# Sinkhorn attention followed by a two-layer feed-forward net on one core: the first dense layer begun early, pieces of the second layer's queue moved next to each other, one copy moved to another engine

**Chip, cores, metric.** One core of one Trainium2 chip. The time is device microseconds of that core, the median of several executions. A ratio is the mean time of one kernel's fast runs over the mean of the other kernel's fast runs of the same rounds, so it is not quite the ratio of the medians that are quoted.

## The reference

Four batches, eight heads, 768 positions, head width 64. Keys and values are mixed across eight blocks of 96 positions with a matrix P (five rounds of row and column normalising), attention is computed inside each block, and the result goes through a feed-forward net with 2048 inner features.

```python
k_sorted = np.einsum('bhij,bhjcd->bhicd', P, k_b).reshape(B, H, S, D)
v_sorted = np.einsum('bhij,bhjcd->bhicd', P, v_b).reshape(B, H, S, D)
scores = scale * np.matmul(q_b, k_sb.transpose(0, 1, 2, 4, 3))
attn = np.exp(scores - max) / sum
x = np.matmul(attn, v_sb)              # -> [3072, 512]
h = x @ w_in
r = np.maximum(h, 0.0)
out = (s * (r * r) + b) @ w_out
```

## The kernel before

TensorE does nearly everything, and the program fixes its order by hand. Each batch has two tiles (t = 2b and 2b + 1, 384 rows of x each). `ffn1(t)` is the first dense layer of a tile (tiles `hps`, `rt`, `gt`), `ffn2(t)` the second (`ops`, `ot`). While the second layer of one batch runs, a `Queue` slips in small pieces of the attention of the next, one piece after every four `ops` products:

- K pieces (`tk`, `ks`) mix keys; S pieces (`sc`, `at`) make scores and exponentials; P pieces (`pv`, `x`) apply them to the values; V pieces (`tv`, `vn`) mix values; q pieces (`tq`, `qt`) transpose q.
- K and S pieces use 64 of TensorE's 128 rows (forms 64\*128 and 64\*96 in the profile); `ops`, `hps`, q pieces and the V pieces of these queues use 128.
- A piece ends with copies out of PSUM on VectorE ("v") or ScalarE ("s").

```python
psa = ctx.enter_context(tc.tile_pool(name="psa", bufs=3, space=bass.MemoryType.PSUM))  # K, S, P, q, V2, hps
psb = ctx.enter_context(tc.tile_pool(name="psb", bufs=2, space=bass.MemoryType.PSUM))  # ops and small pieces

def k_piece(b, c0, nc2, nb, eng):
    pr = brows(b)[1] if nb == 1 else slice(0, 128)
    ...
        ps = psa.tile([128, nc2, nb * 64], FP, tag="a", name="tk")
    for c in range(nc2):
        nc.tensor.matmul(out=ps[:, c, :],
                         lhsT=kb[pr, c0 + 2 * c:c0 + 2 * c + 2, :].rearrange("p c d -> p (c d)"),
                         rhs=rhs, start=True, stop=True)
    ...                                # four casts into ks on engine eng

def bias_piece():                      # bias; then the first results of ffn2 may leave PSUM
    bps = psa.tile([128, 2, 512], FP, tag="a", name="bps")
    nc.tensor.matmul(out=bps[:, 0], lhsT=onesf, rhs=csum, start=True, stop=True)
    nc.vector.tensor_scalar(out=bias, in0=bps[:, 0], scalar1=b_bc, scalar2=None, op0=ALU.mult)
    ready.append(True)
    flush()

...                                    # end of the attention of tile 0
        warm_up(2, psa)
    t_part(0, 2, "v", 0, 2)
    warm_up(2, psa)
...
    V2 = [lambda c0=c0: v_piece2(c0, "s") for c0 in range(0, BLK, 16)]
    qu = Queue([nothing, lambda: q_piece(1, 2, "v")]
               + [lambda c0=c0: k_piece(1, c0, 16, 1, "vsv"[c0 // 32])() for c0 in range(0, BLK, 32)]
               + [seq(lambda: load_q(2), lambda: load_k(*brows(2)), bias_piece), V2[0], S2(2, 0), V2[1], S2(2, 2), V2[2], V2[3],
                  P2(2, 0), V2[4], P2(2, 2), V2[5], S2(3, 0),
                  seq(T(2), K(2, 0, 16, "s")), P2(3, 0), S2(3, 2), K(2, 32, 16, "s"), P2(3, 2), T(3),
                  seq(lambda: q_turn(2), K(2, 64, 16, "s"))], 24)
    ffn2(0, qu)
    ffn2(1, qu)
```

`load_q(2)` is six loads of 128 KB, `load_k` one of 768 KB; GpSimd issues both, after the `csum` sums that the bias needs. I call the queue above the **first queue** (second layer of batch 0) and the next one the **second queue** (second layer of batch 1).

The softmax here doesn't subtract the row's maximum and nothing guards it: scores larger than these inputs give would overflow.

Of the kernel before, what the change touches and what calls it, by code (L numbers as in the profile page):

```python
# [18 lines left out]
def kernel(  # L19
# [74 lines left out]
    def load_k(rows, prow, n=1):  # L94
        for c0 in range(0, BLK, BLK // n):
            cs = slice(c0, c0 + BLK // n)
            nc.gpsimd.dma_start(out=kb[prow, cs, :], in_=kraw[rows, cs, :])
# [4 lines left out]
    def brows(b):  # L102
        return slice(b * 64, (b + 1) * 64), slice((b % 2) * 64, (b % 2) * 64 + 64)
# [75 lines left out]
    def warm_up(n, pool=psb):  # L179
        wp = pool.tile([128, 256], FP, tag="b" if pool is psb else "a", name="wp")  # L180
        for _ in range(n):
            nc.tensor.matmul(out=wp, lhsT=zt[:, 0:128], rhs=zt, start=True, stop=True)  # L182
# [61 lines left out]
    def q_half(half, eng):  # L244

        if half == 0:
            QT[0] = qtp.tile([128, NHP, S], BF, tag="qt", name="qt0")
        pr = slice(half * 64, half * 64 + 64)
        ps = psa.tile([128, 2, 1024], BF, tag="a", name="tq")
        for hp in range(NHP):  # L250
            for t in range(TQ):
                c0 = (hp % 2) * TG + t * 64
                for e in range(2):
                    nc.tensor.transpose(out=ps[e * 64:(e + 1) * 64, hp // 2, c0:c0 + 64],  # L254
                                        in_=qr[0][pr, 2 * hp + e, t, :], identity=ident[pr, pr])
        for a in range(2):
            evac(QT[0][:, 2 * a:2 * a + 2, half * TG:(half + 1) * TG].rearrange(
                     "q b (p t) -> q b p t", t=TQ),
                 ps[:, a, 0:2 * TG].rearrange("q (b t p) -> q b p t", b=2, t=TQ), eng)

    def q_piece(b, hp0, eng):

        if hp0 == 0:
            QT[b] = qtp.tile([128, NHP, S], BF, tag="qt", name=f"qt{b}")
        ps = psa.tile([128, 2, 1024], BF, tag="a", name="tq")
        for i in range(2):
            for t in range(TQ):
                for e in range(2):
                    nc.tensor.transpose(
                        out=ps[e * 64:(e + 1) * 64, i, t * 128:(t + 1) * 128],  # L270
                        in_=qr[b][:, 2 * (hp0 + i) + e, t, :], identity=ident)
        evac(QT[b][:, hp0:hp0 + 2, :].rearrange("q a (p t) -> q a p t", t=TQ),
             ps[:, :, 0:S].rearrange("q a (t p) -> q a p t", t=TQ), eng)
# [8 lines left out]
    def k_piece(b, c0, nc2, nb, eng):  # L282




        pr = brows(b)[1] if nb == 1 else slice(0, 128)
        rhs = (pd1[pr] if b < 2 else pd2[pr, b - 2]).rearrange("p e m i -> p (e m i)")
        if nc2 * nb > 8:
            ps = psa.tile([128, nc2, nb * 64], FP, tag="a", name="tk")  # L290
        else:
            ps = psb.tile([128, nc2, nb * 64], FP, tag="b", name="tk")
# [4 lines that stand above are left out]
        g0 = (b % 2) * 32  # L297

        def half(cp):
            if b == 0:  # L300
                cs = slice(c0 + cp, c0 + 2 * nc2, 2)
            else:
                cs = slice(cp * (BLK // 2) + c0 // 2, cp * (BLK // 2) + c0 // 2 + nc2)
            for e in range(2):
                evac(ks[e * 64:(e + 1) * 64, g0:g0 + nb * 32, cs].rearrange(
                         "p (b g) c -> p b g c", b=nb),
                     ps[cp * 64:(cp + 1) * 64].rearrange(
                         "p c (b e g) -> p e b g c", b=nb, e=2)[:, e], eng)

        half(0)  # L310
        return lambda: half(1)
# [69 lines left out]
    def p_piece(t, hp, n0=0, nn=HB):  # L381
# [15 lines left out]
        for e in range(2):  # L397
# [11 lines left out]
            in0=pvv[:, :, :, 0:D],  # L409
            in1=rec[:, :, 0:nn].unsqueeze(3).broadcast_to([BLK, 2, nn, D]), op=ALU.mult)  # L410

    def t_piece(t, eng, n0=0, nn=HB):

        x = X[t]
        if t not in XT:
            XT[t] = xtp.tile([128, NHP, TG], BF, tag="xt", name="xt")
        if nn < HB:
            t1 = psb.tile([128, 1024], BF, tag="b", name="tr")
            tr = [t1[:, hp * nn * BLK:(hp + 1) * nn * BLK] for hp in range(NHP)]
            src = t1[:, 0:NHP * nn * BLK]  # L420
            dst = XT[t][:, :, n0 * BLK:(n0 + nn) * BLK]
            src = src.rearrange("p (a t) -> p a t", a=NHP)
        else:
            t2 = psa.tile([128, 2, 1024], BF, tag="a", name="tr")
            tr = [t2[:, hp // 2, (hp % 2) * TG:(hp % 2 + 1) * TG] for hp in range(NHP)]
            src = t2[:, :, 0:2 * TG]
            dst = XT[t].rearrange("p (a b) t -> p a (b t)", b=2)
        for hp in range(NHP):
            for n in range(n0, n0 + nn):
                nc.tensor.transpose(out=tr[hp][:, (n - n0) * BLK:(n - n0 + 1) * BLK],  # L430
                                    in_=x[:, n, hp * 128:(hp + 1) * 128],
                                    identity=ident[0:BLK, 0:BLK])
        evac(dst, src, eng)
# [27 lines left out]
    def nothing():  # L461
        pass

    def ffn1(t, slot=nothing, n0=0, nn=HB):
        if t not in GT:
            GT[t] = gtp.tile([128, NF, TG], BF, tag="gt", name="gt")
        gt = GT[t]
        c0, nt = n0 * BLK, nn * BLK
        for f0 in range(0, NF, 2):
            hps = psa.tile([128, 2, 512], FP, tag="a", name="hps")  # L470
            for f in range(2):
                for hp in range(NHP):
                    nc.tensor.matmul(out=hps[:, f, 0:nt], lhsT=wi_at(hp, f0 + f),  # L473
                                     rhs=xt_at(t, hp, n0, nn),
                                     start=(hp == 0), stop=(hp == NHP - 1))
            rt = rtp.tile([128, 2, TG], BF, tag="rt", name="rt")
            nc.scalar.activation(out=rt[:, :, 0:nt], in_=hps[:, :, 0:nt], func=AF.Relu)  # L477
            nc.vector.tensor_tensor(out=gt[:, f0:f0 + 2, c0:c0 + nt], in0=rt[:, :, 0:nt],  # L478
                                    in1=rt[:, :, 0:nt], op=ALU.mult)
            slot()  # L480
# [59 lines left out]
    def seq(*fs):  # L540
        def run():
            for f in fs:
                f()
        return run

    def S2(t, hp):
        return lambda: (s_piece(t, hp), s_piece(t, hp + 1))

    def P2(t, hp):
        return lambda: (p_piece(t, hp), p_piece(t, hp + 1))  # L550
# [53 lines left out]
            t_part(0, 0, "s", 0, 2)  # L604
        warm_up(2, psa)
    t_part(0, 2, "v", 0, 2)
    warm_up(2, psa)

    load_v(*brows(2))

# [1 line left out]
    def P(t, hp, *r):  # L612
        return lambda: p_piece(t, hp, *r)

    def SC(t, hp):
        return lambda: s_piece(t, hp)

    def V1(i, eng="s"):
        return lambda: v_piece1(i * 8, eng)

    ffn1(0, Queue([P(0, 0, 2, 2), P(0, 1, 2, 2), P(0, 2, 2, 2), P(0, 3, 2, 2),
                   lambda: q_half(1, "s"), lambda: t_piece(0, "v", 2, 2), SC(1, 0), SC(1, 1)], 8), 0, 2)
    ffn1(0, Queue([seq(SC(1, 2), P(1, 0)), V1(0), seq(SC(1, 3), P(1, 1)), V1(1), P(1, 2), P(1, 3),
                   seq(V1(2), V1(3)), lambda: t_piece(1, "v")], 8), 2, 2)
    V1(4)()
    V1(5)()
# [20 lines left out]
    def K(b, c0, nc2, eng):  # L647
        return lambda: k_piece(b, c0, nc2, 1, eng)()

    V2 = [lambda c0=c0: v_piece2(c0, "s") for c0 in range(0, BLK, 16)]  # L650
    qu = Queue([nothing, lambda: q_piece(1, 2, "v")]
               + [lambda c0=c0: k_piece(1, c0, 16, 1, "vsv"[c0 // 32])() for c0 in range(0, BLK, 32)]
               + [seq(lambda: load_q(2), lambda: load_k(*brows(2)), bias_piece), V2[0], S2(2, 0), V2[1], S2(2, 2), V2[2], V2[3],
                  P2(2, 0), V2[4], P2(2, 2), V2[5], S2(3, 0),
                  seq(T(2), K(2, 0, 16, "s")), P2(3, 0), S2(3, 2), K(2, 32, 16, "s"), P2(3, 2), T(3),
                  seq(lambda: q_turn(2), K(2, 64, 16, "s"))], 24)
    ffn2(0, qu)
    ffn2(1, qu)

# [6 lines left out]
    v_read(3, nc.gpsimd)  # L666
    load_q(3)
    qu = Queue([S2(4, 0), nothing, nothing, P2(4, 0), nothing, S2(4, 2), nothing, nothing,
                P2(4, 2), nothing, T(4), K(3, 0, 16, "v"), S2(5, 0), nothing, K(3, 32, 16, "s"),
                P2(5, 0), nothing, S2(5, 2), nothing, P2(5, 2), K(3, 64, 16, "s"), T(5),  # L670
                lambda: q_turn(3), nothing], 24)
    ffn2(2, qu)
    ffn2(3, qu)
# [39 lines left out]
```

## Time and profile before

| | before |
|---|---|
| time, median (range) | 233.32 us (233.07 to 233.37) |
| span in the profile | 231.6 us |
| TensorE busy | 224.3 us, 97% |
| VectorE / ScalarE / GpSimd busy | 50% / 49% / 21% |
| mean granted TensorE clock | 0.971 |

The chain that ended last, by engine, shows how much of the set time was not TensorE's own. ("q" after a name is the engine's sequencer.)

```profile
PE 82%; DVE 7%; DMA 5%; ACT 3%; issue 1%; POOL 0%; POOLq 0%
```

DVE's 7% is mostly the stretch that holds up the first results of the second layer. On TensorE's timeline it is one gap. The columns are start us, length us, engine, line, operation, out<-in, form, element type, count, and in brackets how long TensorE had been idle and what ended that.

```profile
69.18 0.73 PE L375 MATMUL sc<-qt,ks 64*96 64x96 bf16 x16
70.32 1.02 PE L516 MATMUL ops<-wo,gt 128*128 128x512 bf16 x4 [0.41 <-DVE ot L490]
```

A score block that should occupy 0.49 us occupies 1.14, because the next `ops` product needs a PSUM buffer that the first `ot` on VectorE frees. Throughout, I read **starts** of TensorE blocks: the lengths of matmuls are modelled and overlap what follows.

### The profile page before, as it was taken

How to read it: one execution, taken by the hardware profiler on the slowest of the kernel's cores; microseconds unless marked ns; L12 is line 12 of the kernel's file. 1: busy time of each engine (PE TensorE's matmuls, PEld its weight loads, DVE VectorE, ACT ScalarE, POOL GpSimd, SP SyncE). 2: the span in 40 equal slices, each digit the busy share in tenths (PEclk: the TensorE clock that was granted, in tenths of full speed). 3: DMA queues.
4: the chain of work that ended last, by engine and by line, in shares of the span. 5: the costliest groups of instructions: out<-in, count | busy, mean ns of one | idle time of the engine just before them, and what ended most of it. 6: DMA issues, size and time to landing. Idle time of an engine off the chain costs nothing.

```text
span 231.6 us, 4837 instructions
## 1 busy us (share of the span) xinstructions
PE 224.3 (97%) x2036; PEld 136.8 (59%) x2036; DVE 116.8 (50%) x245; ACT 114.6 (49%) x164; POOL 48.3 (21%) x62
## 2 busy tenths in 40 slices
PE   8879999999999999999999999999999999999994
PEld 6779887765544555566555555665555556554442
DVE  5778566638992645244446653343452634432221
ACT  6168479685158486856630645656222236660000
POOL 7820000399992000007920000000000000000000
PEclk9975699999999999999999999999999999999999
DMA  5999999998799992764999995610115240001212
GB/s 93 142 200 211 226 193 205 231 220 183 106 110 180 273 312 63 161 82 65 130 148 133 183 197 115 93 47 0 46 47 113 93 110 4 3 0 45 80 59 91
DMA packets 46695, 28.90 MB, mean 125 GB/s; under 512 B 35921, under 2 KB 41041, under 8 KB 46161
## 3 DMA queue, kind: packets, MB, share of 16 engines
q0 software_dynamic: 18800, 15.21, 47.8%
q1 hardware_dynamic: 27728, 13.32, 26.6%
q8 instruction: 16, 0.26, 0.5%
q10 hardware_dynamic: 144, 0.07, 0.1%
q14 instruction: 7, 0.05, 0.1%
HBM read 29.63 MB, written 8.65 MB: 165 GB/s over the span
## 4 chain that ended last, share of the span: by engine, by line
PE 82%; DVE 7%; DMA 5%; ACT 3%; issue 1%; POOL 0%; POOLq 0%
PE hps L473 35%; PE ops L516 31%; DMA qr<-in_q_dram 5%; PE pv L402 4%; PE sc L375 3%; DVE gt L478 2%; ACT ks L240 2%; DVE ks L238 2%; PE tv L320 2%; PE ops L501 2%; PE tk L294 1%; PE tv L350 1%; PE wp L182 1%; PE tq L254 1%; PE tv L336 1%
## 5 line engine op out<-in xcount | busy, mean ns | idle before, releaser
L473 PE MATMUL hps<-xt,wi 128*128 128x384 bf16 (+1 forms) x576 | 87.1, 309 | 0.3 <-ACT rt L477 0.3
L516 PE MATMUL ops<-wo,gt 128*128 128x512 bf16 x368 | 86.9, 380 | 0.4 <-DVE ot L490 0.4
L473 PEld LDWEIGHTS <-wi 128*128 128x128 bf16 x576 | 54.1, 98 | 30.6 <-issue 1.3
L477 ACT ACTIVATE rt<-hps 128x768 bf16<-128x768 f32 (+1 forms) x72 | 53.1, 741 | 37.4 <-PE hps L473 37.0
L478 DVE TENSOR_TENSOR gt<-rt 128x768 bf16<-128x768 bf16 (+1 forms) x72 | 41.2, 574 | 50.2 <-ACT rt L477 50.0
L516 PEld LDWEIGHTS <-gt 128*128 128x128 bf16 x368 | 33.6, 98 | 37.2 <-issue 1.0
L378 ACT ACTIVATE at<-sc 96x768 bf16<-96x768 f32 x32 | 24.4, 804 | 27.7 <-PE sc L375 27.7
L490 DVE SCALAR_TENSOR_TENSOR ot<-ops,s_bc,bias 128x512 f32<-128x512 f32 x23 | 17.1, 749 | 41.2 <-PE ops L516 41.2
L240 ACT CAST ks<-tk 64x512 bf16<-64x512 f32 (+1 forms) x32 | 18.6, 582 | 10.5 <-PE tk L294 10.2
L407 DVE TENSOR_TENSOR x<-pv,rec 96x512 bf16<-96x512 f32 (+1 forms) x36 | 22.6, 627 | 1.3
L639 POOL TENSOR_TENSOR csum<-csum,wo 128x512 f32<-128x512 f32 x14 | 17.6, 1254 | 1.0
L402 PEld LDWEIGHTS <-at 96*128 96x128 bf16 (+1 forms) x256 | 12.0, 104 | 3.8
L182 PE MATMUL wp<-zt 128*128 128x256 bf16 x86 | 12.9, 311 | 1.1 <-DVE warm L113 1.1
L238 DVE CAST ks<-tk 64x512 bf16<-64x512 f32 (+1 forms) x20 | 13.0, 651 | 1.1 <-PE tk L294 0.8
L402 PE MATMUL pv<-vs,at 96*128 96x66 bf16 (+1 forms) x256 | 13.0, 199 | 0.1
L240 ACT CAST vn<-tv 128x512 bf16<-128x512 f32 (+1 forms) x12 | 9.4, 799 | 7.2 <-PE tv L350 5.0
L375 PEld LDWEIGHTS <-ks 64*96 64x96 bf16 x256 | 8.6, 128 | 5.8 <-issue 5.1
L406 DVE RECIPROCAL rec<-pv 96x8 f32<-96x8 f32 (+1 forms) x36 | 6.9, 192 | 9.5 <-PE pv L402 9.4
L84 POOL DMA_DIRECT2D qr<-in_q_dram x12 | 10.6, 912 | 4.8 <-DMA kb<-in_k_dram 3.1
L375 PE MATMUL sc<-qt,ks 64*96 64x96 bf16 x256 | 10.9, 219 | 0.1
L182 PEld LDWEIGHTS <-zt 128*128 128x128 bf16 x86 | 9.0, 110 | 2.6 <-DVE warm L113 1.1
L294 PEld LDWEIGHTS <-kb 64*128 64x128 bf16 x192 | 6.7, 99 | 3.9 <-issue 3.4
(73 smaller groups left out, 98.4 us busy)
## 6 DMA issues: line engine op xcount, KB each, us to landing
out_dram<-ot SPq DMA_DIRECT2D x23, 256.0 KB, 2.4
kb<-in_k_dram POOLq DMA_DIRECT2D x4, 768.0 KB, 12.2
vb<-in_v_dram POOLq DMA_DIRECT2D x4, 768.0 KB, 19.0
wi<-in_moe_w_in_dram POOLq DMA_DIRECT2D x2, 1024.0 KB, 19.7
wo<-in_moe_w_out_dram POOLq DMA_DIRECT2D x2, 1024.0 KB, 32.6
qr<-in_q_dram POOLq DMA_DIRECT2D x12, 128.0 KB, 13.5
dv<-vn SPq DMA_DIRECT2D x6, 256.0 KB, 7.5
vs<-dv POOLq DMA_DIRECT2D x4, 384.0 KB, 12.7
```

Of the source, the lines that this page charges most:

```text
L182: nc.tensor.matmul(out=wp, lhsT=zt[:, 0:128], rhs=zt, start=True, stop=True)
L238: nc.vector.tensor_copy(out=out, in_=in_)
L240: nc.scalar.copy(out=out, in_=in_)
L375: nc.tensor.matmul(out=sc[:, e, n * BLK:(n + 1) * BLK], lhsT=ks[pr, g0 + n, :], rhs=QT[b][pr, hp, q0:q0 + BLK], start=True, stop=True)
L378: nc.scalar.activation(out=at, in_=sc[:, :, 0:TG], func=AF.Exp, scale=scale)
L402: nc.tensor.matmul(out=pv[e][0:m, (n - n0) * VW:(n - n0 + 1) * VW], lhsT=atf[:, c0:c0 + m], rhs=VS[b][:, gi, :], start=True, stop=True)
L407: nc.vector.tensor_tensor(out=x[:, n0:n0 + nn, hp * 128:(hp + 1) * 128].rearrange("p n (e d) -> p e n d", e=2), in0=pvv[:, :, :, 0:D], in1 ...
L473: nc.tensor.matmul(out=hps[:, f, 0:nt], lhsT=wi_at(hp, f0 + f), rhs=xt_at(t, hp, n0, nn), start=(hp == 0), stop=(hp == NHP - 1))
L477: nc.scalar.activation(out=rt[:, :, 0:nt], in_=hps[:, :, 0:nt], func=AF.Relu)
L478: nc.vector.tensor_tensor(out=gt[:, f0:f0 + 2, c0:c0 + nt], in0=rt[:, :, 0:nt], in1=rt[:, :, 0:nt], op=ALU.mult)
L516: nc.tensor.matmul(out=ops, lhsT=gt[:, f, m * 128:(m + 1) * 128], rhs=wo_at(f), start=(f == 0), stop=(f == NF - 1))
L639: nc.gpsimd.tensor_tensor(out=csum, in0=csum, in1=wo_at(f), op=ALU.add)
```

## The change

Its intent: (1) do useful products in place of two dummy warm-up products ahead of the first dense layer; (2) take a wait for a relu away; (3) put pieces that use 64 rows directly behind each other, so that TensorE changes its tiling (the form in which its rows and columns are divided) less often; (4) move the q copy from busy VectorE to idle ScalarE, so that bias and the first `ot` come earlier. An added function `p_pair` is never called and is left out here.

```diff
-    def ffn1(t, slot=nothing, n0=0, nn=HB):
+    def ffn1(t, slot=nothing, n0=0, nn=HB, lead=0):
 ...
+        for f0 in range(0, lead, 2):
+            begun[f0] = psa.tile([128, 2, 512], FP, tag="a", name="hps")
+            products(f0, begun[f0], range(0, NHP // 2))
         for f0 in range(0, NF, 2):
+            if f0 in begun:
+                hps = begun[f0]
+                products(f0, hps, range(NHP // 2, NHP))
 ...
     t_part(0, 2, "v", 0, 2)
-    warm_up(2, psa)
 ...
-                   lambda: q_half(1, "s"), lambda: t_piece(0, "v", 2, 2), SC(1, 0), SC(1, 1)], 8), 0, 2)
-    ffn1(0, Queue([seq(SC(1, 2), P(1, 0)), V1(0), seq(SC(1, 3), P(1, 1)), V1(1), P(1, 2), P(1, 3),
+                   lambda: q_half(1, "s"), lambda: t_piece(0, "v", 2, 2), SC(1, 0), SC(1, 1)], 8), 0, 2, 2)
+    ffn1(0, Queue([seq(SC(1, 2), P(1, 0)), V1(0), seq(SC(1, 3), P(1, 1)), P(1, 2), V1(1), P(1, 3),
 ...
-    qu = Queue([nothing, lambda: q_piece(1, 2, "v")]
-               + [lambda c0=c0: k_piece(1, c0, 16, 1, "vsv"[c0 // 32])() for c0 in range(0, BLK, 32)]
-               + [seq(lambda: load_q(2), lambda: load_k(*brows(2)), bias_piece), V2[0], S2(2, 0), ...
-                  P2(2, 0), V2[4], P2(2, 2), V2[5], S2(3, 0),
-                  seq(T(2), K(2, 0, 16, "s")), P2(3, 0), S2(3, 2), K(2, 32, 16, "s"), P2(3, 2), T(3),
-                  seq(lambda: q_turn(2), K(2, 64, 16, "s"))], 24)
+    qu = Queue([nothing, seq(lambda: q_piece(1, 2, "s"), K(1, 0, 16, "v")), nothing,
+                seq(K(1, 32, 16, "s"), K(1, 64, 16, "v")), nothing,
+                seq(lambda: load_q(2), lambda: load_k(*brows(2)), bias_piece),
+                V2[0], S2(2, 0), V2[1], S2(2, 2), V2[2], V2[3], P2(2, 0), V2[4], P2(2, 2), V2[5],
+                seq(T(2), S2(3, 0), K(2, 0, 16, "s")), nothing, P2(3, 0),
+                seq(S2(3, 2), K(2, 32, 16, "s")), nothing, P2(3, 2),
+                seq(T(3), lambda: q_turn(2)), K(2, 64, 16, "s")], 24)
 ...                                     # second queue
-                P2(4, 2), nothing, T(4), K(3, 0, 16, "v"), S2(5, 0), nothing, K(3, 32, 16, "s"),
-                P2(5, 0), nothing, S2(5, 2), nothing, P2(5, 2), K(3, 64, 16, "s"), T(5),
+                P2(4, 2), nothing, T(4), nothing, seq(S2(5, 0), K(3, 0, 16, "v")), nothing, nothing,
+                P2(5, 0), nothing, seq(S2(5, 2), K(3, 32, 16, "s")), nothing, P2(5, 2),
+                K(3, 64, 16, "s"), T(5),
```

More of the change, by code (lines that the diff above doesn't have):

```diff
@@ L410, in p_piece, with p_pair @@
             in1=rec[:, :, 0:nn].unsqueeze(3).broadcast_to([BLK, 2, nn, D]), op=ALU.mult)
+    def p_pair(t, hp0, n0):
+        b, half = divmod(t, 2)
+        if t not in X:
+            X[t] = xp.tile([BLK, HB, d_model], BF, tag="x", name="x")
+        p2 = psa.tile([128, 4, 256], FP, tag="a", name="pv")
+        for i in range(2):
+            atf = AT[t, hp0 + i].rearrange("p e t -> p (e t)")
+            for e in range(2):
+                for n in range(2):
+                    c0 = (e * HB + n0 + n) * BLK
+                    gi = e * 32 + (hp0 + i) * NB + half * HB + n0 + n
+                    nc.tensor.matmul(out=p2[:, 2 * i + e, n * VW:(n + 1) * VW],
+                                     lhsT=atf[:, c0:c0 + 128], rhs=VS[b][:, gi, :],
+                                     start=True, stop=True)
+        pvv = p2[0:BLK, :, 0:2 * VW].rearrange("p a (n w) -> p a n w", w=VW)
+        rec = rtp.tile([BLK, 4, 2], FP, tag="rec", name="rec2")
+        nc.vector.reciprocal(out=rec, in_=pvv[:, :, :, D])
+        nc.vector.tensor_tensor(
+            out=X[t][:, n0:n0 + 2, hp0 * 128:(hp0 + 2) * 128].rearrange(
+                "p n (a d) -> p a n d", d=D),
+            in0=pvv[:, :, :, 0:D], in1=rec.unsqueeze(3).broadcast_to([BLK, 4, 2, D]),
+            op=ALU.mult)
     def t_piece(t, eng, n0=0, nn=HB):
@@ L468, in ffn1, with products @@
         c0, nt = n0 * BLK, nn * BLK
-        for f0 in range(0, NF, 2):
-            hps = psa.tile([128, 2, 512], FP, tag="a", name="hps")
+        begun = {}
+        def products(f0, hps, part):
             for f in range(2):
-                for hp in range(NHP):
+                for hp in part:
                     nc.tensor.matmul(out=hps[:, f, 0:nt], lhsT=wi_at(hp, f0 + f),
@@ L475, in ffn1 @@
                                      start=(hp == 0), stop=(hp == NHP - 1))
+        for f0 in range(0, lead, 2):
+            begun[f0] = psa.tile([128, 2, 512], FP, tag="a", name="hps")
+            products(f0, begun[f0], range(0, NHP // 2))
+        for f0 in range(0, NF, 2):
+            if f0 in begun:
+                hps = begun[f0]
+                products(f0, hps, range(NHP // 2, NHP))
+            else:
+                hps = psa.tile([128, 2, 512], FP, tag="a", name="hps")
+                products(f0, hps, range(NHP))
             rt = rtp.tile([128, 2, TG], BF, tag="rt", name="rt")
@@ L650 @@
     V2 = [lambda c0=c0: v_piece2(c0, "s") for c0 in range(0, BLK, 16)]
-    qu = Queue([nothing, lambda: q_piece(1, 2, "v")]
-               + [lambda c0=c0: k_piece(1, c0, 16, 1, "vsv"[c0 // 32])() for c0 in range(0, BLK, 32)]
-               + [seq(lambda: load_q(2), lambda: load_k(*brows(2)), bias_piece), V2[0], S2(2, 0), V2[1], S2(2, 2), V2[2], V2[3],
-                  P2(2, 0), V2[4], P2(2, 2), V2[5], S2(3, 0),
-                  seq(T(2), K(2, 0, 16, "s")), P2(3, 0), S2(3, 2), K(2, 32, 16, "s"), P2(3, 2), T(3),
-                  seq(lambda: q_turn(2), K(2, 64, 16, "s"))], 24)
+    qu = Queue([nothing, seq(lambda: q_piece(1, 2, "s"), K(1, 0, 16, "v")), nothing,
[5 more added lines that the diff above has]
+                seq(T(3), lambda: q_turn(2)), K(2, 64, 16, "s")], 24)
     ffn2(0, qu)
```

## The prediction

> **What bounds the kernel now.** I read the page first. TensorE is busy nearly all the time, so the time is TensorE's instruction stream plus the few places where it stands still, and anything on another engine counts only if it makes TensorE stand still.
>
> ```profile
> span 231.6 us, 4837 instructions
> ...
> PE 224.3 (97%) x2036; PEld 136.8 (59%) x2036; DVE 116.8 (50%) x245; ACT 114.6 (49%) x164; POOL 48.3 (21%) x62
> ```
>
> Busy TensorE still hides two costs, so I went to TensorE's timeline and took starts only (ends are modelled and overlap the next start). The columns are start, length, engine and line, operation, out<-in.
>
> ```profile
> 79.75 1.03 PE L516 MATMUL ops<-wo,gt 128*128 128x512 bf16 x4
> 80.62 0.59 PE L350 MATMUL tv<-vb,pd 128*128 128x512 bf16 x2
> 81.05 1.03 PE L516 MATMUL ops<-wo,gt 128*128 128x512 bf16 x4
> 82.01 0.56 PE L375 MATMUL sc<-qt,ks 64*96 64x96 bf16 x16
> 82.50 1.04 PE L516 MATMUL ops<-wo,gt 128*128 128x512 bf16 x4
> 83.47 0.64 PE L294 MATMUL tk<-pd,kb 64*128 64x64 bf16 x16
> 84.04 1.04 PE L516 MATMUL ops<-wo,gt 128*128 128x512 bf16 x4
> 84.91 0.70 PE L402 MATMUL pv<-vs,at 96*128 96x66 bf16 x16
> ```
>
> Four ops products take 0.87 us when a 128-row piece follows (79.75 to 80.62) but 0.96 or 0.97 when a 64-row piece follows (81.05 to 82.01, 82.50 to 83.47): going into a 64-row piece costs 0.09. Single starts in the trace are 23.5 ns apart inside a score piece and 29.8 ns inside a key piece, so 16 take 0.38 and 0.48, while the blocks take 0.49 and 0.57: coming out costs about 0.10. The first ops gaps after it cost 0.01 more. One excursion into 64-row pieces thus costs **0.20 us**.
>
> The second cost is TensorE's waits. The chain of waits in order of time (start, length, what) shows three that the change touches:
>
> ```profile
> 42.45 0.50 ACT rt L477
> ...
> 61.48 1.67 DVE qt L238
> ...
> 68.73 0.76 DVE bias L561
> ...
> 69.52 0.76 DVE ot L490
> ...
> 70.32 1.02 PE ops L516 x4
> ...
> 85.92 0.59 ACT ks L240
> ...
> 86.55 0.56 PE sc L375 x16
> ```
>
> At 42.45 the hps product waits for a relu; the product before it ended a 0.23 us piece at 42.47 and it starts at 42.99, some 0.47 later than a free one. From 57 to 70 us the chain runs through VectorE: q copy, eight key casts, bias, first ot. The score block at 69.18 takes 1.14 us until 70.32 instead of 0.49: **0.65 us** lost. At 86.55 a score piece has waited 0.14 for a key cast on ScalarE.
>
> **What the Trainium skill says.** "TensorEngine Tiling (Array Packing)", Key Properties: "Changing tiling mode (not just tile) drains the TensorE". The trace agrees, with the 0.09 in and 0.10 out above; score and value pieces that alternate at 21 to 23 us, both 64-row, show no such gap. "SBUF — State Buffer", SBUF: two separate sides: VectorE instructions with two SBUF inputs and GpSimd instructions that read SBUF lock each other out. The trace agrees in kind: gt takes 0.56 us at 49.43 and 1.33 at 54.63 under the csum sums of GpSimd, which is why VectorE comes to its q copy only at 61.5. "TensorE: Matmul & The Clock Gate", Part 1: the clock is released on a free-running activity window, not by the kernel. In this trace the granted clock is 0.50 from 24.0 to 27.7 and 1.00 from 27.8. "DMA: Bandwidth & Descriptors", Queues, rings and completion order: each DMA engine takes turns between the queues that have work. This bears on a rival below.
>
> **The change part by part.**
>
> *First dense layer begun early.* Only one tile (two f) is begun on head pairs 0 and 1; p_pair is defined but never called.
>
> ```profile
> 26.57 0.53 PE L443 MATMUL tr<-ident,x 96*128 96x96 bf16 x4
> 26.90 0.63 PE L182 MATMUL wp<-zt 128*128 128x256 bf16 x2
> 27.32 1.05 PE L473 MATMUL hps<-xt,wi 128*128 128x192 bf16 x8
> 28.20 0.30 PE L402 MATMUL pv<-vs,at 96*128 96x66 bf16 x4
> ```
>
> The two warm-ups from 26.90 to 27.32 go. The four products on pairs 0 and 1 start at 26.90 (ScalarE's copy of that half is done at 26.87), 0.16 each at half clock, until 27.54; VectorE's copy of the other half is done at 27.49, so no wait. The 0.42 us saved is half-clock time: by 27.77 before had done 2.8 of 8 products, after has done 5.4, so it gains 2.6 at 0.083: **0.24 us**, if the clock rises at the same moment. The second half of wi landed at 30.4 (issued 7.9, 22.5 to landing), and is then asked for at 30.6 instead of 30.84: just in time.
>
> *v and value pieces swapped.* The wait of 0.47 goes, but P(1,2) now stands where V1(1) had given ScalarE and VectorE 0.4 us, so the next hps product should wait some 0.2 for the buffer of P(1,1). I count **0.2**.
>
> *Second layer, batches 1 and 2.* q and the first key piece share one excursion, but between two tilings there is still one drain: 0.12. Two key pieces together save one excursion: 0.20. The q copy (1.67 on VectorE, 1.44 as such a copy took at 47.19 on ScalarE) goes to an engine that idled from 59.0 to 63.8. VectorE then does two key pieces (8 casts, some 5.3 us) from 61.1: bias at about 66.4 to 67.2, first ot done by 68.0. TensorE wants that buffer at about 68.9, so the 0.65 is gone with some 0.9 to spare. Sum so far 0.24 + 0.2 + 0.12 + 0.20 + 0.65 = **1.4 us** at the score piece S2(3,0), which then starts at 80.6 instead of 82.0.
>
> *Key pieces behind score pieces.* Two in this queue and two in the next: 4 x 0.21 = 0.85, and the 0.14 at 86.55. In the second queue nothing waits, before or after: its inputs have landed (the transposes of q for batch 2 even go one place earlier). If nothing new waits, the sum is 1.4 + 0.85 + 0.14 = 2.4 us: 230.9.
>
> **The rivals.**
>
> *A. The key load takes the place of the waits removed.* K(2,0) needs the load of batch 2's keys:
>
> ```profile
> L97 POOL DMA_DIRECT2D kb<-in_k_dram x1: 594/594/594, 70.1 to 70.1; - x1
> ...
> DMA to landing us min/median/max: 12.3/12.3/12.3
> ```
>
> Issued at 70.15, landed at 82.4; before asks at 83.47, so 1.05 us of slack. The change asks right behind S2(3,0), at 80.6 + 0.4 = 81.0. Two things take the slack: 1.4 us of gain and one slot of four ops products. The load sits behind six q loads of small packets which follow the csum sums on GpSimd, perhaps 0.4 earlier after; but the DMA queues are full from 62 to 82 us and the ot and v stores come earlier too, so I expect it to land between 81.5 and 82.8, not a microsecond earlier. TensorE would then stand still for about 1.2 us. Sum for landing L: K starts at L + 0.05; the four ops products it used to follow are still to be done (0.86), so the gain there is 83.47 - L - 0.91. With L = 82.2 this is 0.36, and with what follows (0.14 + 0.21 + 0.43) it makes 1.14. I hold this the likeliest, 8 in 10.
>
> *B. ScalarE becomes the bound.* A score piece followed by a key piece puts 1.5 + 2.35 us on it at once, with three PSUM buffers all taken; the next value piece comes 1.7 us later, and the next score piece some 3.5. For: ScalarE is busy 20 of the 34 us from 58 to 92. Against: value pieces need the exponentials alone, which go first. At most 0.3 per place, so 231.5 to 232.5 with the other gains.
>
> *C. No gain at the start*, if the clock rises a window later or wi's second half lands later: lost 0.24 to 0.5, mostly hidden anyway if A holds, since the load sets the time in the middle.
>
> **Range and chances.** 233.3 - 1.1 = 232.2 with A; 230.9 without. Weighted with 8 to 2 the middle is 231.9; B may take some back, so I say **232.1**. The low end 230.8 is all gains with no new wait; the high end 233.2 is a load that lands at 82.8 or later and a wait on ScalarE. Two per cent is 4.7 us, twice the whole sum of gains: faster 0.03, same 0.95, slower 0.02.
>
> **What would show it.** First hps at 26.9 with four products ahead of the second copy; value piece at about 27.96. No 0.65 gap after the first score piece of batch 1 (the block about 0.49 long). Excursions of q with tk, tk with tk and sc with tk, with the second piece's first start about 0.03 behind in the like tilings and about 0.12 behind in q with tk. Under A, TensorE's weight load of tk waits for the DMA of kb by some 1.2 us at 81 to 82. I am wrong if that wait is absent (then near 230.9), if the load lands past 83 (then no gain), or if merged 64-row pieces still cost 0.09 each.

## The result, and the profile after

The median is **233.0 us** (232.95 to 233.38) against 233.34 for the kernel before in the same rounds (233.07 to 233.47): ratio 0.999 with a 95% interval of 0.9973 to 1.0008. Within 2%, inside the forecast range, but the gain is 0.3 us where 1.2 was forecast. All outputs were correct.

```profile
span 231.2 us, 4813 instructions
...
PE 222.2 (96%) x2014; PEld 136.6 (59%) x2034; DVE 115.8 (50%) x244; ACT 115.9 (50%) x165; POOL 48.2 (21%) x62
...
PE 91%; ACT 3%; DVE 3%; issue 1%; DVEq 0%
```

The busy time of TensorE fell by 2.1 us, the span by 0.4. Some 1.1 us of the 2.1 is only that 20 `ops` records are missing from this trace, so busy time can't say how much came back as standing still. I followed the starts of the same blocks in both traces:

| block start (us) | before | after | lead of the changed kernel |
|---|---|---|---|
| first `ops` of the second layer, batch 0 | 57.956 | 57.468 | 0.49 |
| S2(3,0), score piece | 82.007 | 80.556 | **1.45** |
| P2(3,0), value piece behind K(2,0) | 84.912 | 84.806 | **0.11** |
| S2(3,2), score piece | 86.548 | 86.301 | 0.25 |
| P2(3,2), value piece behind K(2,32) | 89.452 | 89.471 | -0.02 |
| first `hps` of tile 4 (behind the second queue) | 140.465 | 140.127 | 0.34 |
| last `ops` | 228.013 | 227.675 | 0.34 |

The gain was there, and it was lost at two places in 9 us. First what worked. The dense layer starts early, without the warm-ups:

```profile
26.49 0.49 PE L467 MATMUL tr<-ident,x 96*128 96x96 bf16 x4
26.84 1.07 PE L498 MATMUL hps<-xt,wi 128*128 128x192 bf16 x8
27.75 0.30 PE L402 MATMUL pv<-vs,at 96*128 96x66 bf16 x4
```

q and key piece follow each other, and the score block before the second layer's first `ot` is no longer held up (68.37 to 68.86 is 0.49):

```profile
59.29 0.86 PE L269 MATMUL tq<-ident,qr 128*64 128x128 bf16 x24
60.08 0.64 PE L294 MATMUL tk<-pd,kb 64*128 64x64 bf16 x16
...
68.37 0.56 PE L375 MATMUL sc<-qt,ks 64*96 64x96 bf16 x16
68.86 1.04 PE L552 MATMUL ops<-wo,gt 128*128 128x512 bf16 x4
```

Then what was lost, from the same timeline:

```profile
80.56 0.56 PE L375 MATMUL sc<-qt,ks 64*96 64x96 bf16 x16
82.50 0.64 PE L294 MATMUL tk<-pd,kb 64*128 64x64 bf16 x16 [1.38 <-ACT at L378]
83.07 1.90 PE L552 MATMUL ops<-wo,gt 128*128 128x512 bf16 x8
84.81 0.70 PE L402 MATMUL pv<-vs,at 96*128 96x66 bf16 x16
...
86.30 0.56 PE L375 MATMUL sc<-qt,ks 64*96 64x96 bf16 x16
87.16 0.64 PE L294 MATMUL tk<-pd,kb 64*128 64x64 bf16 x16 [0.30 <-DVE x L407]
87.73 1.90 PE L552 MATMUL ops<-wo,gt 128*128 128x512 bf16 x8
```

K(2,0) should start about 0.39 after the score piece's start, K(2,32) likewise. The first starts 1.94 later: 1.55 too much. The second starts 0.86 later: 0.46 too much. In the view of waits (engine, operation and line <- releaser; us in total, times, longest) and of the tile `kb`, between 60 and 95 us, two releasers are named for the first of these waits:

```profile
PEld L294 <- DMA kb<-in_k_dram: 1.5, 1, 1.5
PE tk L294 <- ACT at L378: 1.4, 1, 1.4
...
L97 POOL DMA_DIRECT2D kb<-in_k_dram x1: 592/592/592, 69.7 to 69.7; - x1
DMA to landing us min/median/max: 12.7/12.7/12.7
```

By these views the weight load of TensorE waits for the keys, the matmul for the exponentials. In the records the key load landed at 82.453 and the second exponential's semaphore was set at 82.491; the weight load began at 82.495. The two candidates end 38 ns apart, and this trace alone can't say which one mattered. The weight load begins 42 ns after the landing but only 4 ns after the exponential, which is a hint and no more: at other waits below, the lag is 42 ns too.

Two more things are needed to read the times. **Clock.** In the 14 profiles the granted clock is lifted from 0.5 at some moment between 25.9 and 28.9 us, in both kernels. Runs fall into two groups, mean clock about 0.978 and 0.970 (after: 232.95, 232.97, 233.04 at 0.978, and 233.38 at 0.971). In the runs of before beside the three sets of experiments the groups are 0.3 to 0.5 us apart on average and overlap. This profile of after had the clock at 26.80, that of before at 27.77: some 0.2 of the lead of 0.49 at 57 us is that, not the change (from the transposes to the first `ops`, before took 31.39 us, and b_kfirst, the same program up to there, 31.17 with the clock up at 26.88). Another 0.08 is that the transposes themselves began earlier. **Same phase.** From the transposes to the first value piece of the dense layer, before took 1.631 us with the clock up at 27.77, and a kernel with the changed start (a_kfirst_k32) 1.447 with the clock up at 27.74: the early start is worth 0.18. With the clock up at 26.8 to 26.9, b_kfirst took 1.416 against 1.265 (after) and 1.223 (a_k0), thus 0.15 to 0.19.

### The profile page after: what moved, and what is told of

It reads as the page before. It is cut to its first block, busy times and chain, and to the rows that moved or that the text cites. A ratio compares the mean times of both kernels' runs of the same rounds, so it can differ in the third digit from the quotient of the medians.

```text
span 231.2 us, 4813 instructions
## 1 busy us (share of the span) xinstructions
PE 222.2 (96%) x2014; PEld 136.6 (59%) x2034; DVE 115.8 (50%) x244; ACT 115.9 (50%) x165; POOL 48.2 (21%) x62
## 4 chain that ended last, share of the span: by engine, by line
PE 91%; ACT 3%; DVE 3%; issue 1%; DVEq 0%
PE hps L498 36%; PE ops L552 34%; PE wp L182 5%; PE pv L402 4%; PE sc L375 3%; PE tk L294 2%; PE tv L320 2%; PE ops L537 2%; ACT ks L240 1%; DVE x L407 1%; PE tv L350 1%; PE tq L254 1%; ACT at L378 1%; ACT qt L240 1%; ACT rt L513 1%
## 5 line engine op out<-in xcount | busy, mean ns | idle before, releaser
L552 PE MATMUL ops<-wo,gt 128*128 128x512 bf16 x348 | 82.9, 379 | 1.1 <-issue 0.2
L514 DVE TENSOR_TENSOR gt<-rt 128x768 bf16<-128x768 bf16 (+1 forms) x72 | 41.7, 581 | 49.5 <-ACT rt L513 49.3
L552 PEld LDWEIGHTS <-gt 128*128 128x128 bf16 x368 | 34.1, 98 | 37.8 <-issue 0.6
L182 PE MATMUL wp<-zt 128*128 128x256 bf16 x84 | 13.5, 328 | 1.1 <-DVE warm L113 1.1
L406 DVE RECIPROCAL rec<-pv 96x8 f32<-96x8 f32 (+1 forms) x36 | 6.9, 193 | 10.9 <-PE pv L402 10.9
L294 PE MATMUL tk<-pd,kb 64*128 64x64 bf16 x192 | 7.1, 190 | 1.7 <-ACT at L378 1.4
```

Source lines behind the costliest of these rows:

```text
L182: nc.tensor.matmul(out=wp, lhsT=zt[:, 0:128], rhs=zt, start=True, stop=True)
L514: nc.vector.tensor_tensor(out=gt[:, f0:f0 + 2, c0:c0 + nt], in0=rt[:, :, 0:nt], in1=rt[:, :, 0:nt], op=ALU.mult)
L552: nc.tensor.matmul(out=ops, lhsT=gt[:, f, m * 128:(m + 1) * 128], rhs=wo_at(f), start=(f == 0), stop=(f == NF - 1))
```

## The experiments

**Theories.** *Theory 1*: K(2,0) waits for the key load, so the gains ahead of it are swallowed by an event with a time of its own. *Theory 2*: it waits for a PSUM buffer that the second exponential of the score piece gives back, so that a key piece directly behind a score piece always waits that long (rival B of the prediction). A third question was the smaller wait of K(2,32).

### The key load before the q loads, in the changed kernel

```diff
-                seq(lambda: load_q(2), lambda: load_k(*brows(2)), bias_piece),
+                seq(lambda: load_k(*brows(2)), lambda: load_q(2), bias_piece),
```

> The changed kernel with one edit: the load of batch 2's keys is issued ahead of the six loads of its q. Theory 1 (the key load took the gain): in the changed kernel the first key piece of batch 2 waited 1.5 us for that load, which landed at 82.45. Issued first it should land some 5 us sooner, so the key piece starts about 0.03 us behind the score piece, at about 81.0, and the whole gain of 1.45 us at that point comes through: about 231.5 us against 233.0 for the change, with 0.46 us still lost at the next key piece, which waits for a PSUM buffer that VectorE frees. Theory 2 (a PSUM buffer): the same key piece could not start before the second exponential of the score piece ahead of it, which ended at 82.49 in the changed kernel, since three buffers are all taken. Then the load does not matter: the key piece still starts about 1.5 us behind the score piece and the time stays at 233.0.

Measured: 231.98 us (ratio 0.9924, 0.9905 to 0.9943), one slow run left out.

```profile
80.52 0.56 PE L375 MATMUL sc<-qt,ks 64*96 64x96 bf16 x16
80.92 0.63 PE L294 MATMUL tk<-pd,kb 64*128 64x64 bf16 x16
...
84.74 0.56 PE L375 MATMUL sc<-qt,ks 64*96 64x96 bf16 x16
85.57 0.64 PE L294 MATMUL tk<-pd,kb 64*128 64x64 bf16 x16 [0.27 <-DVE x L407]
...
L97 POOL DMA_DIRECT2D kb<-in_k_dram x1: 543/543/543, 64.4 to 64.4; - x1
DMA to landing us min/median/max: 9.9/9.9/9.9
```

The keys land at 74.4, and K(2,0) follows the score piece without a wait (80.52 to 80.92, 42 ns behind its last product). The exponentials are what they were. **Theory 2 is dead, theory 1 stands.** K(2,32) still waits 0.43: that wait is another. The time I had expected, 231.5, was not met by the median, 231.98; the profiled run, 231.33, is the fastest of the six.

### The same edit in the kernel before

The edit is the same line of the old queue.

> The kernel before with the same edit. Its first key piece of batch 2 came 1.05 us after the load had landed, so under theory 1 the earlier load is worth nothing here: 233.3, within 0.1 of the kernel before. If this is faster by over 0.5 us, the order of the loads helps for another reason, and the run above says nothing about the change.

Measured: 233.26 (0.9986, 0.9969 to 1.0002). The keys landed at 74.2 instead of 82.4, and the stretch from the start of the first `ops` to that of the last took 170.05 us against 170.06. An earlier landing alone is worth nothing; it is worth a microsecond only together with the change.

### K(2,32) one slot later

```diff
-                seq(S2(3, 2), K(2, 32, 16, "s")), nothing, P2(3, 2),
+                S2(3, 2), K(2, 32, 16, "s"), P2(3, 2),
```

> The changed kernel with the second key piece of batch 2 put one slot behind its score piece instead of directly behind. In the changed kernel it waited 0.46 us for a PSUM buffer that VectorE freed at 87.12. One slot later (0.97 us) this wait should be gone, for one more excursion into 64-row pieces (0.21): a gain of 0.25, so 232.75, and the products after the queue start 0.25 sooner with respect to the landing of the key load. If the time stays at 233.0 or grows, the wait was hidden or moves to the next piece.

Measured: 233.17 (0.9989, 0.9961 to 1.0016), with a wide spread (232.62 to 234.85) that leaves the time undecided. In the profile the wait is gone: K(2,32) starts 1.46 behind its score piece, as in before.

```profile
86.21 0.56 PE L375 MATMUL sc<-qt,ks 64*96 64x96 bf16 x16
86.70 1.04 PE L552 MATMUL ops<-wo,gt 128*128 128x512 bf16 x4
87.67 0.64 PE L294 MATMUL tk<-pd,kb 64*128 64x64 bf16 x16
```

K(2,0) still waits for the load (82.36 landed, 82.41 started). The stretch from the first `ops` of the second layer to the first `hps` of tile 2, which contains the whole first queue, took 34.46 us against 34.93. Below I call it the **queue stretch**; in before it was 34.42.

Not all of these 0.47 are the edit's: 0.20 lie ahead of K(2,0), which started 24.83 us after the first `ops` here and 25.03 in after, with the landing of its load. From the start of K(2,0) to the end of the stretch it is 9.64 us against 9.90: 0.26 gained, as expected (0.25). That is the wait of 0.46 less the 0.20 that the merge saves. **A key piece merged with a score piece cost more than it gave at this place**: the key piece needs the third PSUM buffer while VectorE still reads it for x of P(3,1), which ended at 87.117 in the trace of after; the weight load of K(2,32) began at 87.159, again 42 ns later. In after_again, a_kfirst and a_k0 the lag behind the same instruction is 42 or 43 ns too. No run changed the number of buffers: that it is a buffer is read from the program and the trace.

### The early start alone

```diff
 # in the kernel before: ffn1 with lead as in the change, called with lead=2 for tile 0
-    warm_up(2, psa)
```

> The kernel before with the early start of the first dense layer alone. Theory: it is worth 0.24 us at the same phase of the clock, and comes through in full, since the kernel before has 1.05 us of slack ahead of its key load: 233.1 against 233.35. If the key load's slack is smaller than seen, or the clock's phase decides all, no difference from the kernel before.

Measured: 233.63 (0.9997, 0.9977 to 1.0016): nothing. The trace, of the slowest of the six runs (233.93), shows the gain swallowed twice:

```profile
83.47 0.64 PE L294 MATMUL tk<-pd,kb 64*128 64x64 bf16 x16 [0.39 <-ACT at L378]
...
117.87 0.69 PE L402 MATMUL pv<-vs,at 96*128 96x66 bf16 x16 [0.47 <-DMA vs<-dv]
...
DMA to landing us min/median/max: 13.7/13.7/13.7
```

The second layer began 0.48 earlier, but the key load of this run landed at 83.42 and K(2,0) started at 83.465, as in before (83.47). What was left was lost when a value piece of batch 2 waited for its values: landed 117.733 here, asked for about 117.24. In the profile of before that load landed at 116.695, before it was asked. Again the trace names an exponential for the first wait, but that one ended at 83.471 (its semaphore was set at 83.480), after K(2,0) had started (83.465): here the name in the view is plainly wrong, and the landing (83.419, weight load 42 ns after) is what remains.

### Both repairs of the changed kernel

The two edits above together: key load first, K(2,32) one slot later.

> Both edits on the changed kernel: the key load first, and the second key piece of batch 2 one slot behind its score piece. With the load first alone the products after the queue started at 90.80 us, and the second key piece still waited 0.43 for a PSUM buffer. That wait goes, one excursion comes back (0.21): the products should start 33.15 us after the first ops product, against 33.37, and the whole be some 0.2 us faster than with the load first alone, 0.9915 of the kernel before. If the wait only moves to the next value piece, no change.

Measured: **231.42 us** (231.24 to 231.94; ratio 0.9917, 0.9899 to 0.9934), the best of all kernels run.

```profile
84.94 0.56 PE L375 MATMUL sc<-qt,ks 64*96 64x96 bf16 x16
85.43 1.04 PE L552 MATMUL ops<-wo,gt 128*128 128x512 bf16 x4
86.40 0.64 PE L294 MATMUL tk<-pd,kb 64*128 64x64 bf16 x16
86.97 1.04 PE L552 MATMUL ops<-wo,gt 128*128 128x512 bf16 x4
```

Neither key piece waits; the queue stretch is 33.14 us, where 33.15 was expected. Out of the gain, 1.28 us is this stretch (34.42 less 33.14).

### K(2,0) one slot later, old order of loads

```diff
-                seq(T(2), S2(3, 0), K(2, 0, 16, "s")), nothing, P2(3, 0),
+                seq(T(2), S2(3, 0)), K(2, 0, 16, "s"), P2(3, 0),
```

> The changed kernel with the first key piece of batch 2 moved back one slot, so that four ops products stand between it and its score piece, the loads in their old order. If the landing of the load (82.4) sets the start of the key piece, it still starts at about 82.5, but four ops products (0.86 us) are done before it instead of after it: 0.8 to 0.9 us faster than the change, some 232.2, and the wait ahead of it is 0.5 instead of 1.5. If it was the place behind the score piece as such that cost (a PSUM buffer), the wait would be gone altogether and the piece would start at 82.0.

Measured: 232.11 (0.9964, 0.9926 to 1.0002).

```profile
80.93 0.56 PE L375 MATMUL sc<-qt,ks 64*96 64x96 bf16 x16
81.42 1.04 PE L552 MATMUL ops<-wo,gt 128*128 128x512 bf16 x4
82.57 0.64 PE L294 MATMUL tk<-pd,kb 64*128 64x64 bf16 x16
...
DMA to landing us min/median/max: 12.4/12.4/12.4
```

The keys landed at 82.52 and K(2,0) started at 82.57, but four `ops` products were done in the time in which after stood still. The block of these four took 1.15 instead of 0.97: a wait of 0.18. The time is what was expected, 232.2; the interval touches 1, so its size is told by the trace more than by the time.

### The q copy on ScalarE alone

```diff
-    qu = Queue([nothing, lambda: q_piece(1, 2, "v")]
+    qu = Queue([nothing, lambda: q_piece(1, 2, "s")]
```

> The kernel before with the q copy of batch 1 on ScalarE alone. Theory: VectorE reaches the bias some 1.1 us sooner and the 0.65 us in which the ops product waited for the first ot are gone, so the first key piece of batch 2 asks at 82.8 instead of 83.47, still after a landing at 82.4: the 0.65 come through, 232.7. If the load lands later than 82.8 in a run, it takes part of that. If the wait for ot does not shrink, the chain through VectorE was not set by the q copy.

Measured: 232.65 (0.9967, 0.9951 to 0.9984). One letter gives at least as much as the whole change (0.999 in its own rounds, 0.9981 when run again; the intervals overlap, so that it gives more is not shown).

```profile
68.99 0.56 PE L375 MATMUL sc<-qt,ks 64*96 64x96 bf16 x16
69.55 1.02 PE L516 MATMUL ops<-wo,gt 128*128 128x512 bf16 x4
```

The score block takes 0.56 (more exactly 0.558) where it took 1.14; 0.07 of the wait is left. K(2,0) still comes a slot after the score piece, at 82.70, and the keys landed at 81.77: no new wait, so the gain is kept. In a run whose keys land as late as in b_lead (83.42) most of it would have been lost.

### The swap alone

```diff
-    ffn1(0, Queue([seq(SC(1, 2), P(1, 0)), V1(0), seq(SC(1, 3), P(1, 1)), V1(1), P(1, 2), P(1, 3),
+    ffn1(0, Queue([seq(SC(1, 2), P(1, 0)), V1(0), seq(SC(1, 3), P(1, 1)), P(1, 2), V1(1), P(1, 3),
```

> The kernel before with the value and v piece swapped alone. Read off the traces of before and after, the swap gains 0.15 us by the second v pair (the 0.47 wait goes, a 0.27 one comes) and then 0.12 are lost at the first product of the next first layer, which waits for VectorE's copy of the transposed x. So 0.04 in all: the same time as before, and the stretch from the first score piece of the second half to the first product of 384 columns shorter by under 0.1 us. My prediction had 0.2.

Measured: 233.41 (0.9994, 0.9977 to 1.0011). From the score piece ahead of it to the first product over 384 columns the trace has 10.641 us against 10.686 in before: 0.045 gained. The wait of 0.47 at 42.99 goes and one of 0.27 comes at 40.98, and 0.11 is lost when that first product waits for VectorE's copy of the transposed x.

### The second queue alone

The edit is the last hunk of the diff.

> The kernel before with the changed queue of batches 2 and 3 alone (two key pieces directly behind score pieces). The traces of the change show 47.72 us from the first product of the third first layer to that of the fifth, against 48.08 before: 0.36 us, where my prediction had 0.43. Nothing waits for a load there, so alone it should give the same 0.36: 0.9985 of the kernel before. If less comes, it too meets a load that lands late (the value blocks of batch 2, with 0.55 us of slack before).

Measured: 232.98 (0.9979, 0.9966 to 0.9992). From the first `hps` of tile 2 to that of tile 4 the trace has 47.73 us against 48.08: 0.35. Two saved changes of tiling at 0.20 make 0.40; K(3,32) waits some 0.05. (The time shows 0.5; all its runs were of the group with the higher clock.)

### The changed kernel again

No edit, another chip.

> The changed kernel unchanged, to have more of its runs and its trace a second time beside the others of this chip. 0.9985 to 0.999 of the kernel before; the first key piece of batch 2 again starts 42 ns behind the landing of its load and over a microsecond behind its score piece; the second one waits 0.4 to 0.5 for its buffer.

Measured: 232.99 (0.9981, 0.9964 to 0.9998).

```profile
81.30 0.56 PE L375 MATMUL sc<-qt,ks 64*96 64x96 bf16 x16
81.92 0.64 PE L294 MATMUL tk<-pd,kb 64*128 64x64 bf16 x16
```

In this profile (clock up late, at 28.71) the score piece started at 81.302 and the keys landed at 81.872; K(2,0) started at 81.919, so it waited only 0.22, and K(2,32) waited 0.47 again. I had expected the start over a microsecond behind the score piece; it was 0.62, as both the question and the landing moved. What held is that the start lies 40 to 50 ns behind the landing. Here K(2,0) began before either exponential of its score piece had ended (82.53 and 83.23): in the changed kernel itself, without any edit, that speaks against theory 2. And the landing sets what follows: this profile was 0.74 us behind that of after at the first `ops`, but its keys landed 0.58 earlier, and it was 0.57 ahead at the last.

### The key load made later, in both kernels

```diff
+    spare = const.tile([128, 2, H, D], BF)
 ...
-    seq(lambda: load_q(2), lambda: load_k(*brows(2)), bias_piece)
+    # two more loads of 128 KB, parts of q of batch 2 into spare, between load_q(2) and load_k
```

> The kernel before with two spare loads of 128 KB ahead of the key load of batch 2, which should push its landing out by some 1.8 us, to about 84.2. The kernel before asks for it at 83.43, so the first key piece should wait some 0.8 us: 234.2 against 233.4. If the time does not move, the slack was larger than I read.

> The changed kernel with the same two spare loads. It has no slack, so the whole delay of the landing shows in the first key piece's start: some 1.8 us, 234.8, and more than in the kernel before by 1 us. If the theory of the load were wrong, both kernels would move alike.

Measured in the kernel before: 233.91 (1.0019, 0.9994 to 1.0044, one slow run left out): the landing moved only 0.7, to 83.14, and K(2,0), asking at 83.8, did not wait. Measured in the changed kernel: 239.38 (1.0264, 1.0238 to 1.029). The keys landed at 87.78, 5.3 later than in after, so TensorE stood still for 6.1 us, and then its clock fell. First the timeline, then the landing in before and after with spare loads (the key load alone), then windows (columns: window, length; busy us with counts of PE, PEld, DVE, ACT, POOL; granted clock; DMA share; GB/s):

```profile
81.38 0.56 PE L375 MATMUL sc<-qt,ks 64*96 64x96 bf16 x16
87.82 1.03 PE L294 MATMUL tk<-pd,kb 64*128 64x64 bf16 x16 [5.88 <-DMA kb<-in_k_dram]
```

```profile
DMA to landing us min/median/max: 10.9/10.9/10.9
```

```profile
DMA to landing us min/median/max: 15.5/15.5/15.5
```

```profile
82.00:87.00 5.00, 0.00 (x0) 0.00 (x0) 0.00 (x0) 1.30 (x2) 0.00 (x0) 0.99 1.02 247
87.00:93.70 6.70, 5.66 (x41) 3.30 (x43) 0.72 (x2) 2.32 (x4) 0.00 (x0) 0.50 0.54 102
```

The weight load of K(2,0) began 42 ns behind the landing, now that the exponentials had been done for more than four microseconds: the landing is the releaser. Both sizes I had expected were missed (0.8 and 1.8 us): I can't set the landing time by adding loads. But the two kernels answer as theory 1 says: the one with a slot between does not stand still, the other waits for whatever moment the load lands. The long wait also cost a second time in this run: TensorE's last start ahead of it is at 81.73, the granted clock fell to 0.50 at 86.95 and stayed there until 93.77, and from K(2,0) to the first `hps` of tile 2 it took 12.2 us instead of the 9.9 of after, although K(2,32) no longer waited.

**What stays open.** With the old order the same 768 KB load was issued at 69.7 to 70.5 us in nine profiles, and landed at 79.4 to 83.4. These are eight different kernels, one of them twice (after and after_again, 82.45 and 81.87), so how far one kernel varies is not shown. I did not find what sets that moment. DMA is full in that window (in before, share 1.06 from 74.5 to 79 us and 1.02 from 79 to 82.4), and six q loads stand before it in GpSimd's queue, but no run separates these. The turns between queues, which the prediction cites from the Trainium skill, are shown by no run here. Loading keys first made it land at 73.8 to 74.4 in three profiles.

## Why the prediction was right or wrong

**Right: what bounds the kernel, and that the load takes the place of the waits.** Rival A was held likeliest, 8 in 10, and it happened: K(2,0) waited for its keys (after, and by the key-first runs), and 1.45 us of lead at S2(3,0), forecast as 1.4, shrank to 0.11. That 1.45 meets 1.4 is in part luck. From the first `ops` to S2(3,0) the change gained 0.96 (23.09 against 24.05 us, in after_again 23.09 too), where 0.12 + 0.20 + 0.65 = 0.97 was forecast; but of the 0.49 ahead of that, where 0.44 was forecast, some 0.2 are the clock and 0.08 the earlier transposes.

**Right in kind and size.** The 0.65 wait for the first `ot` went completely (block 0.49). A saved change of tiling is worth 0.20 (in b_second 0.35 gained and 0.05 waited for two; in a_k32 a wait of 0.46 less 0.26 gained for one). Where nothing waits, a key piece follows a score piece 42 to 45 ns, and a key piece 29 ns, after the last start (0.03 forecast), with q to K at 0.15 (0.12 forecast). The 0.14 at S2(3,2) was gained (0.11 became 0.25).

**Where it failed: the terms of rival A's sum.** The step was "with L = 82.2 this is 0.36, and with what follows (0.14 + 0.21 + 0.43) it makes 1.14".

| term of that sum | forecast | measured in after | why |
|---|---|---|---|
| 83.47 - L - 0.91 | 0.36 | 0.11 | L was 82.45 |
| wait at S2(3,2) | 0.14 | 0.14 | |
| merge of K(2,32) | +0.21 | -0.27 | +0.20 saved, 0.46 waited for a PSUM buffer |
| second queue | 0.43 | 0.36 | two merges of 0.20, a wait of 0.05 |
| sum | 1.14 | 0.34 | |

The largest wrong term is K(2,32): 0.48 of the 0.80. Rival B had seen that three PSUM buffers would all be taken, but named **ScalarE** and said "at most 0.3 per place"; the buffer was held by **VectorE's** x of P(3,1), for 0.46, and the sum for A had no term for it at all. That unmerging it gives back 0.26 in a_k32 (from K(2,0) on) and 0.24 in a_kfirst_k32 (queue stretch 33.14 against 33.37 in a_kfirst) shows this term to be the right one. The second wrong term is L: a landing that lies anywhere within 4 us in nine profiles of several kernels was given as 81.5 to 82.8, and its middle used as if known. The 0.25 error in it is small beside that spread, so it was partly the luck of the profile: in after_again it landed at 81.87, and that profiled run took 232.37.

**Small, and wrong twice over.** The swap brought 0.04 instead of 0.2 (a wait was moved, and another product waited for VectorE), the early start 0.15 to 0.19 instead of 0.24 (the 2.6 products at 0.083 of the forecast make 0.22, not 0.24). Neither changed the total of after, since both stand ahead of the landing; the early start alone showed the same (nothing gained).

**The weighting.** I moved the point from 232.2 to 232.1 for a case without any stall (230.9 at 2 in 10), and let B take back only what was left over. The measured waits of A and B added up. With both repaired, the gain is 2.0 us (231.42 against 233.42 in its rounds), close to the 2.4 of the sum without stalls, less the swap's 0.16 and the merge of K(2,32) that the repair gives up, 0.2.

## What to carry to other kernels

A gain ahead of a transfer with a time of its own is not yet a gain: before a consumer is moved forward, compare its new time of asking with the landing in the trace, for every load behind it, and issue first what is asked for first. Putting two pieces next to each other to save a change of mode takes one more buffer at that moment; count who still reads it. Where two releasers end within 40 ns, don't trust the name in the view: look whether the named one had ended at all when the wait was over, then move one of them, and see whether the start follows.

## What the Trainium skill lacked or had wrong

- "TensorEngine Tiling (Array Packing)", Key Properties, says that a change of tiling mode drains TensorE but not what it costs. Here: 0.09 us into a 64-row piece, 0.10 out, 0.20 for an excursion. Score (64\*96) and key (64\*128) pieces, which differ in columns only, followed each other 42 to 45 ns after the last start, so no drain of that size shows between them.
- "Perfetto Trace Analysis", Per-instruction lifecycle, says that the propagation of semaphores is not in the profile, but gives no length there. Here TensorE's weight load began 42 ns after what released it, behind a landing (82.453 to 82.495) and behind VectorE (87.117 to 87.159); ten such waits in six profiles give 41 to 43 ns.
- No page that I read has a figure for how far the landing of one load spreads while the queues are full. Here the same 768 KB load, issued within 0.8 us in nine profiles of eight kernels, landed within a range of 4 us (79.4 to 83.4), and with the same two more loads ahead of it took 10.9 us in one kernel and 15.5 in another.
